# A planned DeltaNet and FFN kernel on one core: the planner learns of the eight transfers that may be open

## The chip, the cores and the metric

The kernel runs on one core of one Trainium2 chip. The metric is the device time of one execution in microseconds. It is given as the median of several runs; the profile is of one execution.

## The reference

Two layers follow each other. The first is a DeltaNet recurrence over 768 steps, for 4 batches of 8 heads of 48 dimensions; the second is a SwiGLU feed-forward network (FFN) without bias on the 3072 resulting tokens of 384 numbers, with 1536 inner columns and an RMS norm ahead of it.

```python
k_n = k / (norm(k) + 1e-6)
for t in range(S):
    y[t] = q[t] @ state
    v_old = state.T @ k_n[t]
    state = state + beta[t] * outer(k_n[t], v[t] - v_old)
x = y.transpose(0, 2, 1, 3).reshape(3072, 384)
xn = x / sqrt(mean(x * x) + 1e-6) * rms_g
out = (silu(xn @ w_gate) * (xn @ w_val)) @ w_out
```

The three weight matrices come in as 64-bit floats, and the kernel turns them into 32-bit ones itself.

## The kernel before

**Work.** The 768 steps are cut into twelve chunks of 64 (`C`). For each chunk `c`, `prep(c)` makes the small triangular matrix that replaces the 64 sequential steps, `qpart(c)` makes the masked scores of queries against keys, and `recur(c)` applies both to the state and gives the chunk's 256 rows of `x`. Then the FFN works on these 256 tokens. Chunks 0 and 1 go through `ffn_plain` (up-products L1083, down-products L1065); chunks 2 to 11 go through `ffn` and `down`, which form the products with fewer multiplications from sums of weight blocks (L1176 and L1233).

**A chunk's chain.** In `prep`, the keys' scores go to DRAM (`dkk`) and come back in another layout as `at`. VectorE (DVE) scales it (L654), takes a first share (L679, L684, L689) and does 15 steps of two instructions (L701 and L707). The result goes to DRAM as `dx`, and for chunks 2 to 11 also as `dxt`, and comes back in four transfers of `x2bd` and eight of `mt`, and for chunks 2 to 11 two of `m1bd`. TensorE (PE) merges the blocks (L783, L807; for chunks 0 and 1 also L759), with short copies by DVE (L772, L823) and ScalarE (ACT) in between; `recur` follows with L894, L908 and L945, DVE's copy L933 and the transposes L1016 that give `xf`, the FFN's input. For chunks 0 and 1 the result lies in `wsum`.

**Weights.** `weights` loads 18 blocks of 768 KB into three raw buffers in `more`; each is turned into 32-bit floats by one ACT instruction (L465) and three or four DVE ones (L453, L456, L461, and L486 where PE doesn't add the parts).

**Order.** Nothing of the order is left to the compiler. Each operation is an `Op` of the class `Plan`, with an engine, a duration, a priority and its dependences. `Plan.run` calls `forward` and `backward` by turns, 60 times (`ROUNDS`), with small random shakes of the priorities from a fixed seed, and keeps the order whose modelled end is the earliest. `forward` is a list scheduler: among the operations whose dependences are met, it takes the one with the earliest start and, among equal starts, the smallest key. `backward` sets the keys anew from the latest times at which each operation may start. The chosen order is then issued; each engine works through its list in order, and what holds it up on the chip are semaphores alone. The modelled times stay behind, with one exception: where PE's plan has a hole before 70 us, `filler` puts matmuls on the identity there (L1333), as many as fill the hole as planned.

**Transfers in the plan.** `dma` adds a transfer to the list of SyncE (SP) or, for a few of chunk 0, of ACT. The model has one `server` for all transfers: each occupies it for its `work`, after those planned ahead of it, and its dependents can start 0.7 us after its end. Some have an `after`, an earliest time in the plan. The work of a weight block is 3.06 us, of a half of `k`, `q` or `v` 1.02, of a half of `at` 1.8, of an `mt` or `x2bd` transfer 0.3. On the chip a transfer's landing is told by one of eight semaphores, which go round over the transfers of SP and ACT together in the order of the list; a transfer that takes a semaphore again waits until the transfer that used it before has landed. The plan before doesn't know that.

**Ports.** `op.port` marks operations of DVE or POOL that, in the model, can't run beside those of the other engine. `Plan.add` sets it false for every operation of SP and ACT.

Of the kernel before, what the change touches and what calls it, by code (L numbers as in the profile page):

```python
# [62 lines left out]
class Plan:  # L63
# [47 lines left out]
    def forward(self, banks, until):  # L111

        at = dict.fromkeys(ENGINES, 0.0)
        held = {"DVE": 0.0, "POOL": 0.0}
        cand = {e: [] for e in ENGINES}
        free = list(banks)
        for op in self.ops:
            op.wait, op.at = len(op.deps), op.ready
            for g in op.acquire:
                g.taken, g.uses = False, g.left  # L120
            if not op.wait:
                cand[op.eng].append(op)
        order, server, end_, mode = [], 0.0, 0.0, 0
        backlog = 0.0
        while len(order) < len(self.ops):
            best = None
            for e in ENGINES:
                for op in cand[e]:
                    s = max(op.at, at[e])
                    if op.port:  # L130
                        s = max(s, held["POOL" if e == "DVE" else "DVE"])
                    n = sum(not g.taken for g in op.acquire)
                    if n > len(free):
                        continue
                    if n:
                        s = max(s, free[n - 1])
                    key = op.key + (STICK if op.mode is not None and op.mode != mode else 0.0)
                    rate, store = (FETCH, AHEAD) if s > EARLY else (FETCH0, AHEAD0)
                    if op.size and backlog + op.size - rate * op.dur > store:
                        key += 2.0 * STICK  # L140
                    if best is None or (s, key, op.n) < best[0]:
                        best = ((s, key, op.n), op)
            if best is None:
                return None
            (s, _, _), op = best
            cand[op.eng].remove(op)
            for g in op.acquire:
                if not g.taken:
                    g.taken = True
                    free.pop(0)  # L150
            op.start = s
            if op.mode is not None and op.mode != mode:
                s += 0.1
                op.start, mode = s, op.mode
            end = s + op.dur
            if op.eng == "PE":
                if s - at["PE"] > 1.4 and s > until:
                    end += 1.6
                rate, store = (FETCH, AHEAD) if s > EARLY else (FETCH0, AHEAD0)
                fill = 6.0 if s < until else 0.0  # L160
                backlog = max(0.0, backlog - (rate - fill) * (s - at["PE"])) + op.size - rate * op.dur
                late = max(0.0, backlog - store) / rate
                backlog, end = max(0.0, backlog - rate * late), end + late
            at[op.eng] = end - min(OVERLAP[op.eng], op.dur)
            if op.port:
                held[op.eng] = end
            end_ = max(end_, end)
            for g in op.release:
                g.uses -= 1
                if not g.uses:  # L170
                    free.append(end + 0.1)
                    free.sort()
            if op.dma:
                server = max(end + 0.9, server) + op.work
                end = server
            op.end = end
            for u in op.users:
                u.wait -= 1
                u.at = max(u.at, at[op.eng] if u.eng == op.eng and not op.dma else end + op.hop(u) + u.slack)
                if not u.wait:  # L180
                    cand[u.eng].append(u)
            order.append(op)
        self.end = end_
        return order
# [65 lines left out]
def kernel(  # L250
# [17 lines left out]
    nc = tc.nc  # L268
# [94 lines left out]
    G = lambda n: 0.15 + 0.0022 * n  # L363

    def dma(dst, src, prio, r=(), w=(), work=0.3, dur=0.5, eng="SP", after=0.0):
        queue = nc.scalar if eng == "ACT" else nc.sync
        op = P.add(eng, dur, lambda: queue.dma_start(out=dst, in_=src), prio, r, w, lat=0.7)
        op.dma, op.work, op.ready = True, work, after

    PERIOD = 51.0  # L370

# [41 lines left out]
    def load_small():  # L413
        for i in range(8):
            src = beta.rearrange("b (y g) (c i t) -> i g (b y) c t", i=2, g=2, t=W)[i // 2 % 2, i % 2]
            dma(beta_b[16 * i : 16 * i + 16], src, 0.5, w=[("beta", i)], work=0.2, after=7.5)
        dma(g_sb, moe_rms_g.rearrange("(t p) -> p t", p=128), 1, w=["g"], after=8.0)
# [6 lines left out]
    def weights():  # L424
# [14 lines left out]
        for n, (dst, src, keys) in enumerate(todo):  # L439
            pr = (30 if n < 9 else CV2) + 0.2 * n  # L440
            i, a = n % NRAW, n % NCV
            parts = dst.shape[1]
            rdst = raw[i].rearrange("p (a c) -> p a c", a=parts)
            dma(rdst, src, (0.1 if n == 0 else 3 + 2 * n), w=[("raw", i)], dur=0.7, work=3.06, after=(7.5, 5.0, 19.2, 27.2, 24.5, 33.3, 47.0)[n] if n < 7 else 48.8)

            low, high = (raw[i].bitcast(U32)[:, w_ : w_ + 2 * WCOL - 1 : 2] for w_ in range(2))
# [922 lines left out]
```

## Time and profile before

| What | Value |
|---|---|
| Median of 3 runs | 712.54 us (712.05 to 716.23) |
| Span of the profiled execution, first to last instruction | 709.8 us |
| Instructions | 23280 |
| PE busy | 700.7 us (99%) |
| DVE busy | 543.5 us (77%) |
| ACT busy | 314.0 us (44%) |
| POOL busy | 139.9 us (20%) |
| Moved by DMA | 54.66 MB, mean 77 GB/s |
| Mean granted TensorE clock | 1.000 |

The profiled execution is a run of its own, for which the page gives the span and no other time; the span lies 2.7 us under the median of the runs. PE's busy time contains the filler, so it doesn't say how much of PE's time is useful. The share of DVE, and that of the DMA engines, is a mean over a first part with much of both and a long rest with little.

### The profile page before, as it was taken

Reading aid. Unit: us, or ns where it says so; the run is one execution under the profiler, and the core shown is the slowest. Engines: PE = TensorE matmul, PEld = TensorE weight load, DVE = VectorE, ACT = ScalarE, POOL = GpSimd, SP = SyncE. Lnnn points to the kernel's source line nnn. Section 1 sums busy time; section 2 is a strip of 40 time slices with the busy share of each in tenths; the row PEclk is TensorE's granted clock in tenths of the full one; section 3 lists DMA queues with packets and bytes.
Section 4 is the critical chain, followed back from the end, with each engine's and each line's share of the span. In section 5 each row is a group of like instructions: output and inputs, shape, how many; then the busy total and the mean of one; then the engine's idle time right before and its main releaser. Section 6 shows DMA issues by size and latency. Waiting matters only on the chain.

```text
span 709.8 us, 23280 instructions
## 1 busy us (share of the span) xinstructions
PE 700.7 (99%) x10040; PEld 637.8 (90%) x10040; DVE 543.5 (77%) x1138; ACT 314.0 (44%) x732; POOL 139.9 (20%) x140
## 2 busy tenths in 40 slices
PE   8999999999999999999999999999999999999997
PEld 5657868778799999999999999999999999999997
DVE  4899989999679759849969769669679547957373
ACT  5435554233245445445444445346345345245241
POOL 4201211103133132233223133133213003000000
PEclk9999999999999999999999999999999999999999
DMA  7878795341451161162542431442430350040000
GB/s 138 221 149 188 180 262 170 51 79 24 75 112 27 33 111 31 28 111 46 90 77 47 74 71 25 90 76 48 78 67 11 56 103 2 15 64 2 23 1 23
DMA packets 210070, 54.66 MB, mean 77 GB/s; under 512 B 199216, under 2 KB 202288, under 8 KB 209968
## 3 DMA queue, kind: packets, MB, share of 16 engines
q1 hardware_dynamic: 205120, 52.26, 36.9%
q10 hardware_dynamic: 4848, 0.92, 0.8%
q8 instruction: 79, 1.29, 0.8%
q14 instruction: 23, 0.19, 0.1%
HBM read 40.83 MB, written 12.32 MB: 75 GB/s over the span
## 4 chain that ended last, share of the span: by engine, by line
PE 91%; DVE 5%; DMA 3%; issue 1%; ACT 1%; POOL 0%; ACTq 0%; POOLq 0%; DVEq 0%
PE bank L1176 39%; PE bank L1233 19%; PE bank L1083 9%; PE bank L1065 4%; PE bank L538 3%; PE bank L848 3%; PE bank L515 3%; PE bank L1333 2%; PE bank L894 2%; PE bank L908 2%; DMA more<-in_moe_w_gate_dram 2%; PE bank L807 2%; DVE acc L707 1%; PE bank L1016 1%; PE bank L945 1%; DVE acc L701 1%
## 5 line engine op out<-in xcount | busy, mean ns | idle before, releaser
L1186 DVE TENSOR_TENSOR tmp<-tmp,bank 128x512 f32<-128x512 f32 x180 | 121.2, 682 | 79.5 <-PE bank L1176 68.5
L1176 PE MATMUL bank<-xf,w_in 128*128 128x128 f32 x1440 | 181.1, 277 | 0.0
L1176 PEld LDWEIGHTS bank<-xf,w_in 128*128 128x128 f32 x1440 | 170.1, 192 | 2.6 <-issue 0.8
L1176 PE MATMUL bank<-xf,more 128*128 128x128 f32 x960 | 125.2, 277 | 0.0
L1176 PEld LDWEIGHTS bank<-xf,more 128*128 128x128 f32 x960 | 115.4, 192 | 2.4 <-issue 0.6
L1188 ACT COPY tmp<-bank 128x512 f32<-128x512 f32 x120 | 69.0, 586 | 78.2 <-PE bank L1176 58.3
L1192 ACT ACTIVATE tmp<-tmp 128x256 f32<-128x256 f32 x120 | 49.9, 417 | 97.9 <-DVE tmp L1186 97.6
L707 DVE TENSOR_REDUCE acc<-acc 128x30 f32<-128x90 f32 (+4 forms) x180 | 85.1, 473 | 6.2
L560 POOL TENSOR_TENSOR knrm<-ksum,half 128x16 f32<-128x16 f32 x12 | 36.2, 3019 | 158.0 <-DVE ksum L559 158.0
L701 DVE TENSOR_TENSOR acc<-acc,at 128x60 f32<-128x60 f32 (+4 forms) x180 | 62.3, 346 | 2.8
L1233 PE MATMUL bank<-wo_sb,hf 128*128 128x192 f32 x360 | 63.7, 327 | 0.0
L1233 PEld LDWEIGHTS bank<-wo_sb,hf 128*128 128x128 f32 x360 | 58.3, 190 | 0.1
L1193 DVE TENSOR_TENSOR hf<-tmp 128x256 f32<-128x256 f32 x120 | 51.0, 437 | 7.7 <-ACT tmp L1192 7.2
L1333 PE MATMUL bank<-ident 128*128 128x128 f32 (+2 forms) x160 | 44.9, 427 | 1.4 <-POOL ident masks.py:199 1.4
L728 POOL COPY acc<-acc 128x128 f32<-128x128 f32 x40 | 21.5, 568 | 123.1 <-DVE acc L707 122.5
L1333 PEld LDWEIGHTS bank<-ident 128*128 128x128 f32 x160 | 27.0, 196 | 17.9 <-issue 15.2
L654 POOL TENSOR_TENSOR at<-at,beta_b 128x1024 f32<-128x1024 f32 x8 | 18.9, 2360 | 85.7 <-DMA at<-dkk 73.7
L1083 PE MATMUL bank<-xf,w_in 128*128 128x256 f32 x144 | 34.6, 385 | 0.9 <-DVE r L862 0.9
L1065 PE MATMUL bank<-wo_sb,hf 128*128 128x384 f32 x96 | 34.6, 491 | 0.0
L1083 PE MATMUL bank<-xp,w_in 128*128 128x256 f32 x144 | 32.8, 380 | 0.0
L1083 PEld LDWEIGHTS bank<-xf,w_in 128*128 128x128 f32 x144 | 26.4, 190 | 6.0 <-DVE r L862 1.5
L1083 PEld LDWEIGHTS bank<-xp,w_in 128*128 128x128 f32 x144 | 27.0, 190 | 4.6
(166 smaller groups left out, 1024.5 us busy)
## 6 DMA issues: line engine op xcount, KB each, us to landing
at<-dkk SPq DMA_DIRECT2D x23, 256.0 KB, 4.2
q<-in_q_dram SPq DMA_DIRECT2D x24, 192.0 KB, 3.7
more<-in_moe_w_val_dram SPq DMA_DIRECT2D x6, 768.0 KB, 6.2
more<-in_moe_w_gate_dram SPq DMA_DIRECT2D x6, 768.0 KB, 7.4
more<-in_moe_w_out_dram SPq DMA_DIRECT2D x6, 768.0 KB, 6.9
vt<-in_v_dram SPq DMA_DIRECT2D x24, 192.0 KB, 4.2
out_dram<-tmp SPq DMA_DIRECT2D x48, 96.0 KB, 2.2
k<-in_k_dram SPq DMA_DIRECT2D x23, 192.0 KB, 3.8
```

The lines of the kernel that those rows point to most:

```text
L560: P.add("POOL", 2.95, lambda: nc.gpsimd.tensor_tensor(out=knrm[i2], in0=ksum[i2], in1=half, op=ALU.pow), pn, r=[("ksum", i2), "half"], w=[ ...
L701: nc.vector.tensor_tensor(out=acc[:, 1:3, 0:n, j + 2 : W].rearrange("p a i t -> p i a t"), in0=acc[:, old, 0:n, j : j + 2, None].to_broadc ...
L707: nc.vector.tensor_reduce(out=acc[:, new, 0:n, j + 2 : W], in_=acc[:, lo : lo + 3, 0:n, j + 2 : W].rearrange("p a i t -> p i t a"), axis=A ...
L1065: nc.tensor.matmul(po[p].t[:, 0:DM], hf[:, spot(f), 128 * p : 128 * p + 128], wo_sb[:, spot(f)], start=(f == f0), stop=(f == f1 - 1), skip ...
L1083: nc.tensor.matmul(ps.t[:, TOK * side : TOK * side + TOK], w_in[:, side, h_, 3 * t + i_, n : n + 128], x_[:, 2 * t : 2 * t + 2].rearrange( ...
L1176: nc.tensor.matmul(g.t[:, 128 * z : 128 * z + 128], fac[:, side, 128 * f : 128 * f + 128], xf[:, xs], start=(begin and z == 0), stop=False ...
L1186: P.add("DVE", V(512), lambda t=t, g=g: nc.vector.tensor_tensor(out=t, in0=t, in1=g.t, op=ALU.add), -1, r=[g], w=[tk], last=g)
L1188: P.add("ACT", A(512), lambda t=t, g=g: nc.scalar.copy(t, g.t), -1, r=[g], w=[tk], last=g)
L1192: P.add("ACT", A(256), lambda t=t: nc.scalar.activation(out=t[:, 0:256], in_=t[:, 0:256], func=ACTF.Silu), -1, w=[tk])
L1193: P.add("DVE", V(256), lambda t=t, f0=f0, p=p: nc.vector.tensor_tensor(out=hf[:, spot(f0) : spot(f0) + 2, 128 * p : 128 * p + 128], in0=t[ ...
L1233: nc.tensor.matmul(g.t[:, 0:192], a_[:, f], b_[:, f], start=(begin and f == 0), stop=(f == 5), skip_group_check=True)
L1333: nc.tensor.matmul(warm[:, 0 : 128 * w_].rearrange("p (w n) -> p w n", n=128), ident, ident[:, None, :].to_broadcast([128, w_, 128]))
```

## The change

`forward` keeps a list of eight times, one for each of the last eight transfers of SP and ACT in the order of planning: the modelled landing plus 0.7 us. A further transfer of SP or ACT can't start in the plan before the oldest of them. `dma` learns of a third queue, POOL, and sets `op.port` false for each transfer; no call in the kernel names that queue. The code that issues instructions is otherwise as it was, and so are all durations, priorities and the seed; the order comes out of the planner anew.

```diff
@@ forward
         order, server, end_, mode = [], 0.0, 0.0, 0
         backlog = 0.0
+        lanes = [0.0] * 8
         while len(order) < len(self.ops):
             best = None
             for e in ENGINES:
                 for op in cand[e]:
                     s = max(op.at, at[e])
+                    if op.dma and e != "POOL":
+                        s = max(s, lanes[0])
                     if op.port:
                         s = max(s, held["POOL" if e == "DVE" else "DVE"])
...
             if op.dma:
                 server = max(end + 0.9, server) + op.work
                 end = server
+                if op.eng != "POOL":
+                    lanes = lanes[1:] + [end + 0.7]
             op.end = end
@@ dma
-        queue = nc.scalar if eng == "ACT" else nc.sync
+        queue = {"ACT": nc.scalar, "SP": nc.sync, "POOL": nc.gpsimd}[eng]
         op = P.add(eng, dur, lambda: queue.dma_start(out=dst, in_=src), prio, r, w, lat=0.7)
-        op.dma, op.work, op.ready = True, work, after
+        op.dma, op.work, op.ready, op.port = True, work, after, False
```

## Prediction

> **What bounds the kernel now.** First the page's busy shares and slices.
>
> ```profile
> PE 700.7 (99%) x10040; PEld 637.8 (90%) x10040; DVE 543.5 (77%) x1138; ACT 314.0 (44%) x732; POOL 139.9 (20%) x140
> PE   8999999999999999999999999999999999999997
> DVE  4899989999679759849969769669679547957373
> ```
>
> TensorE is busy from end to end, so an order can gain only where that busy time isn't useful work. Next, the windows by stage show which engines are full in each (columns: window, length, busy time and count of PE, PE loads, DVE, ACT, POOL; clock; DMA share; GB/s).
>
> ```profile
> 30.00:40.00 10.00, 10.00 (x35) 5.32 (x34) 9.30 (x20) 2.86 (x5) 0.00 (x0) 1.00 0.88 177
> 60.00:70.00 10.00, 9.87 (x285) 8.16 (x284) 9.52 (x26) 7.08 (x23) 1.82 (x3) 1.00 0.94 147
> 100.00:110.00 10.00, 10.00 (x159) 7.14 (x159) 9.38 (x15) 6.66 (x17) 4.52 (x3) 1.00 1.08 250
> 110.00:160.00 50.00, 50.00 (x585) 39.32 (x586) 48.55 (x92) 16.83 (x36) 3.97 (x5) 1.00 0.40 86
> 250.00:300.00 50.00, 50.00 (x823) 48.32 (x822) 40.79 (x88) 24.20 (x58) 13.36 (x13) 1.00 0.30 55
> ```
>
> There are three stages. Until 72 us no FFN product runs; PE's busy time is mostly filler (L1333: 44.9 us of it), while from 20 us on DVE is 89 to 98% busy and the DMA engines 0.62 to 0.94. From 72 to 160 us PE, DVE and, until 110, the transfers are full together. From 160 us PE alone is: the list of PE's waits between 72 and 709 us holds one entry, `PE bank L1083 <- DVE r L862`, 0.9 us.
>
> Third, SyncE's queue where chunk 0's merge transfers go out (start, length, what).
>
> ```profile
> 44.98 0.54 SPq L367 DMA_DIRECT2D more<-in_moe_w_gate_dram  x1
> 46.37 0.96 SPq L367 DMA_DIRECT2D mt<-dx  x2
> 47.46 5.43 SPq L367 DMA_DIRECT2D x2bd<-dx  x2
> 52.93 0.95 SPq L367 DMA_DIRECT2D mt<-dx  x2
> ```
>
> Two issues of `x2bd` span 5.43 us, though the first takes 1.17 and the second 0.30: between them SyncE stands 3.95 us, until 52.59. The weight load of 44.98 landed 7.6 us later, at 52.57. By the trace's semaphores it is the eighth transfer ahead of that second issue; the eight semaphores go round, and by issue and landing times never more than seven earlier transfers are open at an issue. So the limit that the change writes into the planner is real before it, too. Seven of the 427 issues stand on it clearly, with 11.0 us of queue time in all; six of them lie before 81 us, the seventh (0.17 us) at 256 us. Steady chunks hardly meet it.
>
> Fourth, the chain of waits just ahead of the FFN (start, length, what).
>
> ```profile
> 57.97 0.64 PE bank L1333 x4
> 59.61 1.50 PE bank L1333 x8
> 62.96 0.86 PE bank L1333 x6
> 65.52 2.36 PE bank L1333 x10
> 69.31 1.72 PE bank L1333 x8
> 71.36 0.88 PE bank L1333 x6
> 72.23 2.62 PE bank L1083 x12
> ```
>
> 7.96 us of filler stand on the chain itself. The planner puts filler where its plan has PE idle before 70 us; where the chip is ahead of the plan, real work waits behind filler.
>
> **The change part by part.** It adds and removes no instruction on the chip: `dma` is called with SP or ACT alone, so the new POOL key is never used, and `op.port` is already False for such an op, so its new last assignment alters nothing (exactly 0, under no cover). The one live edit makes the earliest start of an SP or ACT transfer in `forward` also wait for `lanes[0]`. All 427 issues stay on their queues; what can differ is the list order of all five engines, and the filler. Four terms:
>
> 1. *The waits themselves.* The chip's waits on the eighth transfer stay, whatever the planner knows. Only another order can move them: from -3.95 us (SyncE's longest one goes) to +3.95 (another like it arises). I take 0: the first-come rule of `forward` still issues the 44.98 load as soon as SyncE is free and the load's `after` has passed, ahead of the `mt` transfers, which are candidates only when `dx` has landed at 46.22. Behind a wait of this sort stand the other `mt`, `x2bd` and the two weight loads at 53.99 and 54.49 on SyncE, and ACT's own conversion of weights (`ACT w_in L483` sat 6.6 us there).
>
> 2. *Filler.* A planned transfer that starts later moves planned PE work later, and the hole is filled. Least: all 7.96 us of the chain's filler go. Most: SyncE's 3.95 us turn wholly into filler. The plan already lets transfers land one after the other; with the 44.98 load's 3.06 us in that line its last `mt` lands late even without the rule, so little is added: I take +1, nearer to the row with no wait than to the 3.95.
>
> 3. *Weight loads and their conversion.* After 72 us PE has one hole, 0.9 us at 94, behind a load issued at 85.07 that landed 7.14 us later. Least -0.9; most +8.45 (a load landing one full turn later; the one issued at 97.33 took that long). I take +1, near the 0.9 row, since what is late next is DVE's conversion, which has 0.6 us free in each 10 there.
>
> 4. *The 550 us after 160.* Here PE's rate matters. In the chain 8 matmuls of L1176 in a row take 1.09 us and 16 take 1.98, so each further eight cost 0.89 and each break 0.20. Two breaks fewer a chunk to four more, over ten chunks: -4 to +8. I take one more, +2.0: an order drawn anew has no reason to have fewer, and DVE (40.79 of 50) and ACT have room to follow it.
>
> Sum: 0 + 1 + 1 + 2 = +4.0 on a span of 709.8, 713.8. The median of the runs (712.54) is 2.7 above that span, so 716.5. The four terms' ends don't come together; half of them on either side gives the likeliest case its own range, 708.5 to 721.
>
> One rule bears on the plan's picture of the queues. The row first: an `mt` transfer of ACT's queue, issued at 46.28 with 32 KB, landed 6.5 us later, just after SyncE's 768 KB; the middle one of all SyncE's `mt` takes 2.2. So ACT's small transfer had to wait for SyncE's big one, as in the planner's single line. The Trainium skill, page "DMA: Bandwidth & Descriptors", section "Queues, rings and completion order", has each DMA engine turn between the queues packet by packet, which speaks against the new rule's one line of landings: a small transfer from ACT need not wait for a long one from SyncE. By the page the planned waits would be too long by the difference, 4.3 us, all of it filler, and my sum 720.8; by the row it stays 716.5, and I go by the row.
>
> **Rivals.**
>
> *A worse place for the conversions: 725.* A weight conversion is four DVE instructions, 0.55 + 0.56 + 0.96 + 0.96 = 3.03 us (L453, L456, L461, L486 at 69 to 73 us). Between 50 and 68 us DVE does chunk 1's steps (L701, L707), and chunk 0's short copies (L772, L823, L933) are threaded among them. If the plan holds that chunk 0's transfers land later, conversions get threaded ahead of the copies; on the chip all of chunk 0's path, and the first FFN product at 72.23, then waits. Three of them give +9.1; with the +4 above, 712.5 + 13.1 = 725.6, say 725. From +7.1 us in all it is over 1%, so two conversions (6.1) with half of the small terms decide it. For it: DVE is over 93% busy there, so nothing moved ahead is free. Against it: the copies' priorities come from the backward pass and are far ahead of the conversions'. Six give 735.
>
> *The rule sorts the queue better: 705.* Where all transfers wait for the same lane, `forward` chooses by priority instead of by arrival. Then `at<-dkk` could go ahead of the weight load at 16.80 (the first `at` on ACT's queue took 7.2 us to land, the ordinary ones 4.2: 3.0 us) and chunk 0's `mt` ahead of the load at 44.98 (52.57 instead of 49.94, when the second `at` landed: 2.6), and half of the filler goes (4.0): 9.6 us. But DVE's windows from 20 to 110 us add up to 82.4 of 90: 7.6 us free is all that an earlier start can use before DVE is the bound. 712.5 - 7.6 = 705. For it: that cap is not below the bar of 1%. Against it: it needs nearly all of DVE's idle time, and the transfers at 100 us are full as well.
>
> *It does nothing: 712.5.* If the rule never binds on the plan's best order, list and filler stay. Against it: the plan's line has the same burst of twelve transfers at 46 us behind the same long load.
>
> **How the numbers follow.** Likeliest case 0.42 (of it 0.02 over the bar of 1% on the slow side), misplaced conversions 0.38, better sorting 0.16, nothing 0.04. The slow rival is given nearly as much as the likeliest because three of the four terms can lose more than they can gain, and the full DVE before 160 us gives misplaced work back to the end. One per cent, about what a measurement of this kernel can tell from no change, is 705.4 to 719.7: faster 0.16, same 0.42 - 0.02 + 0.04 = 0.44, slower 0.38 + 0.02 = 0.40. The range holds 8 in 10 from 704.5, just under the fast rival, to 733, which leaves out the slow rival's worst, with more than five conversions.
>
> **What would show it.** The first L1083 product should start at 72 to 75 us; at 80 or later the slow rival is true, at 65 the fast one. L1333's 44.9 us of filler should be 44 to 48. PE's idle after 100 us should stay under 1 us, and the busy time of L1176 within 4 us of now. SyncE should still show a stall of 2 to 5 us among chunk 0's `mt` and `x2bd`. The forecast is wrong if PE gets holes of over 1 us between 110 and 200 us, or if a steady chunk comes to take over 1 us more than now.

## The result, and the profile after

The changed kernel takes 718.16 us (median of 4 runs, 716.65 to 722.23) against 712.29 for the kernel before: a ratio of 1.0083, 95% interval 1.0055 to 1.0111. It is slower by 0.8%, within the bar of 1%. The profiled execution of the changed kernel is its slowest, 722.23 us with a span of 719.6; so some 4 of the 9.8 us between the two spans are that run's own, and what matters is what returns in other runs.

The page's busy shares and slices:

```profile
PE 703.8 (98%) x10028; PEld 638.5 (89%) x10028; DVE 547.5 (76%) x1138; ACT 313.0 (43%) x732; POOL 141.4 (20%) x140
PE   8898899999999999999999999989999999999997
DVE  4889789999699859669679569749739949848373
PEclk9999899999999999999999999999999999999999
```

PE's row has dents that it lacked, and the granted clock one at 72 to 90 us. The windows (length, busy time and count of PE, PE loads, DVE, ACT, POOL; clock; DMA share; GB/s) place them:

```profile
60.00:70.00 10.00, 9.25 (x312) 7.80 (x315) 9.46 (x25) 4.86 (x16) 2.31 (x1) 1.00 0.60 141
70.00:80.00 10.00, 5.95 (x44) 4.37 (x36) 9.79 (x15) 6.76 (x20) 3.98 (x4) 0.68 0.70 149
250.00:300.00 50.00, 50.00 (x827) 48.59 (x826) 38.99 (x88) 23.98 (x58) 12.96 (x13) 1.00 0.34 62
450.00:500.00 50.00, 47.99 (x792) 46.10 (x791) 35.66 (x80) 21.77 (x54) 11.21 (x11) 0.97 0.37 67
```

From 70 to 80 us PE has 4 us without work while DVE is full, and the clock is 0.68 on average. SyncE's queue, by contrast, looks as before:

```profile
44.41 0.54 SPq L372 DMA_DIRECT2D more<-in_moe_w_gate_dram  x1
45.78 0.83 SPq L372 DMA_DIRECT2D mt<-dx  x2
47.12 4.76 SPq L372 DMA_DIRECT2D x2bd<-dx  x2
52.27 0.80 SPq L372 DMA_DIRECT2D mt<-dx  x2
```

The same load is issued ahead of the same transfers, and the second `x2bd` waits for it again, 4.16 us by the issue times (3.95 before). The planner knows of the wait now and takes it all the same. Where the time goes is seen on DVE. First before, then after (start, length, what):

```profile
55.93 0.48 DVE L707 TENSOR_REDUCE acc<-acc 128x96 f32<-128x288 f32 x1
56.33 0.84 DVE L772 COPY m1bd<-bank 32x256 f32<-32x256 f32 x2
57.20 0.39 DVE L701 TENSOR_TENSOR acc<-acc,at 128x220 f32<-128x220 f32 x1
```

```profile
56.29 0.48 DVE L712 TENSOR_REDUCE acc<-acc 128x96 f32<-128x288 f32 x1
...
58.73 0.40 DVE L777 COPY m1bd<-bank 32x256 f32<-32x256 f32 x1
...
60.13 0.42 DVE L777 COPY m1bd<-bank 32x256 f32<-32x256 f32 x1
```

Lines are five higher after the change; L777 is L772. Before, chunk 0's two copies go out together behind the fourth step of chunk 1. After, the first goes behind the sixth and the second behind the seventh, and PE's merge needs both: 60.55 instead of 57.17 us, 3.4 us. That is no wait for transfers: all eight `mt` had landed by 55.0 us, and PE's matmuls that the copies read were done at 55.7. The chain of waits goes on like this:

```profile
68.58 0.07 DVE ms L993
...
69.85 0.47 DVE more L458
70.32 0.07 DVE ms L993
...
72.93 0.92 ACT more L470
73.86 0.63 ACT yn L1008 x2
74.48 0.04 issue
74.53 0.92 PE bank L1021 x3
75.44 0.02 issue
75.47 0.38 ACT xf L1025
75.84 0.04 issue
75.89 5.06 PE bank L1088 x12
```

Weight conversions (L458 on DVE, L470 on ACT) stand ahead of chunk 0's last pieces, and the first FFN products, twelve matmuls that took 2.62 us before, take 5.06: they run at half the clock. In windows of 2 us the clock is 1.00 until 72, 0.89, then 0.50 from 74 to 80.

To see how the loss grows, I counted for each matmul its mean spacing in the profile of before, filler as nothing, and read when so much useful PE work was issued:

| Useful PE work, us | before at | after at | later by |
|---|---|---|---|
| 15 | 43.8 | 44.2 | 0.4 |
| 18 | 57.3 | 60.7 | 3.4 |
| 25 | 72.6 | 77.0 | 4.4 |
| 28 | 75.7 | 81.8 | 6.1 |
| 100 | 149.0 | 154.7 | 5.8 |
| 400 | 448.7 | 453.1 | 4.4 |
| 500 | 548.4 | 557.6 | 9.2 |
| 600 | 648.1 | 657.9 | 9.8 |

So 3.4 us come with the copies. The first product starts 3.7 us later (75.89 against 72.23), and the twelve products at half the clock add 2.4 (5.06 against 2.62): together the 6.1 at 28 us. The row at 25 us lies within these products. Chunk 0's own path lost more than that. First before, then after:

```profile
65.24 0.73 ACT L1003 ACTIVATE yn<-bank,rs 128x192 f32<-128x192 f32 x2
66.59 0.73 ACT L1003 ACTIVATE yn<-bank,rs 128x192 f32<-128x192 f32 x2
```

```profile
72.17 0.73 ACT L1008 ACTIVATE yn<-bank,rs 128x192 f32<-128x192 f32 x2
73.76 0.71 ACT L1008 ACTIVATE yn<-bank,rs 128x192 f32<-128x192 f32 x2
```

Its scaled rows end 7 us later. Some 3.6 us of that lie behind the copies: POOL's key norm (L565, 67.69 to 70.96 us) stands ahead of chunk 0's roots, and the pieces above stand ahead of the rows. Before, PE came to its rows only at 67.7 and 70.9 us, behind filler, so that the first product shows no more than 3.7 of the 7.

Later some of the loss is won back, and this run loses 5 us more after 400, where PE has one hole of 2.0 us and one of 0.8, and the clock falls to 0.50 for 3 us behind the first. About half of these 5 us returns elsewhere: counted in the same way, the profiles of three runs below that keep this part of the list (the old start with the new rest, the filler in the holes, POOL alone reordered) lose 2.5 to 2.7 us between 400 and 600, without the 2.0 us hole and at a clock of 1.00.

### The profile page after: what moved, and what is told of

It reads as the page before. It is cut to its first block, busy times and chain, and to the rows that moved or that the text cites. A ratio compares the mean times of both kernels' runs of the same rounds, so it can differ in the third digit from the quotient of the medians.

```text
span 719.6 us, 23217 instructions
## 1 busy us (share of the span) xinstructions
PE 703.8 (98%) x10028; PEld 638.5 (89%) x10028; DVE 547.5 (76%) x1138; ACT 313.0 (43%) x732; POOL 141.4 (20%) x140
## 4 chain that ended last, share of the span: by engine, by line
PE 84%; DVE 9%; issue 2%; POOL 2%; DMA 1%; ACT 1%; SPq 1%; ACTq 0%; POOLq 0%; DVEq 0%
PE bank L1181 35%; PE bank L1238 19%; PE bank L1088 7%; PE bank L1070 4%; PE bank L543 3%; PE bank L853 3%; PE bank L1338 3%; PE bank L520 2%; DVE acc L712 2%; DVE acc L706 1%; PE bank L812 1%; PE bank L913 1%; PE bank L899 1%; PE bank L1021 1%; PE bank L788 1%
## 5 line engine op out<-in xcount | busy, mean ns | idle before, releaser
L1191 DVE TENSOR_TENSOR tmp<-tmp,bank 128x512 f32<-128x512 f32 x180 | 121.2, 684 | 81.0 <-PE bank L1181 74.1
L1181 PE MATMUL bank<-xf,w_in 128*128 128x128 f32 x1440 | 180.1, 277 | 2.0 <-ACT tmp L1193 2.0
L1181 PE MATMUL bank<-xf,more 128*128 128x128 f32 x960 | 126.3, 279 | 0.8 <-DVE tmp L1191 0.8
L565 POOL TENSOR_TENSOR knrm<-ksum,half 128x16 f32<-128x16 f32 x12 | 37.0, 3082 | 235.9 <-DVE ksum L564 235.9
L1338 PE MATMUL bank<-ident 128*128 128x128 f32 (+2 forms) x148 | 43.2, 439 | 1.4 <-POOL ident masks.py:199 1.4
L1338 PEld LDWEIGHTS bank<-ident 128*128 128x128 f32 x148 | 24.9, 196 | 18.4 <-issue 16.1
L1088 PE MATMUL bank<-xf,w_in 128*128 128x256 f32 x144 | 36.7, 404 | 0.5 <-ACT xf L1025 0.5
L1247 DVE TENSOR_TENSOR tmp<-tmp,bank 128x192 f32<-128x192 f32 x30 | 10.5, 350 | 31.2 <-PE bank L1238 31.2
L1088 PEld LDWEIGHTS bank<-xf,w_in 128*128 128x128 f32 x144 | 28.1, 201 | 6.3 <-ACT xf L1025 0.9
L1088 PE MATMUL bank<-xp,w_in 128*128 128x256 f32 x144 | 33.2, 381 | 0.3 <-DVE hf L1096 0.3
```

The source lines that it names most:

```text
L565: P.add("POOL", 2.95, lambda: nc.gpsimd.tensor_tensor(out=knrm[i2], in0=ksum[i2], in1=half, op=ALU.pow), pn, r=[("ksum", i2), "half"], w=[ ...
L1088: nc.tensor.matmul(ps.t[:, TOK * side : TOK * side + TOK], w_in[:, side, h_, 3 * t + i_, n : n + 128], x_[:, 2 * t : 2 * t + 2].rearrange( ...
L1181: nc.tensor.matmul(g.t[:, 128 * z : 128 * z + 128], fac[:, side, 128 * f : 128 * f + 128], xf[:, xs], start=(begin and z == 0), stop=False ...
L1191: P.add("DVE", V(512), lambda t=t, g=g: nc.vector.tensor_tensor(out=t, in0=t, in1=g.t, op=ALU.add), -1, r=[g], w=[tk], last=g)
L1338: nc.tensor.matmul(warm[:, 0 : 128 * w_].rearrange("p (w n) -> p w n", n=128), ident, ident[:, None, :].to_broadcast([128, w_, 128]))
```

## The experiments

Two theories stood against each other. **The rule**: orders planned with knowledge of the eight transfers are late on the chip. **The draw**: `Plan.run` keeps the best of 60 shaken rounds, and any edit of the planner draws 60 others; the loss is the luck of this draw. Beside that, the start had to be told from the rest, and the pieces of the start from each other.

**Other draws.** The only edit is the seed, in the changed planner or in the one before:

```diff
-        rng = random.Random(47)
+        rng = random.Random(46)   # 62; without the rule: 45, 57
```

The modelled ends of 24 seeds, which the planner itself works out, run from 701.0 to 708.4 us without the rule and from 702.9 to 708.2 with it; the seed in use gives 701.2 and 704.7, so it is a good draw in the first and a middling one in the second. The other seeds that were run are the two with the earliest modelled end in each planner.

> The planner with the new rule, but the shakes of its 60 rounds drawn from seed 46 instead of 47. The planner's own modelled end is 702.9 us instead of 704.7, and its first FFN product stands at 71.0 us instead of 73.6. Theory 'the draw' (the rule costs little, the one order drawn with seed 47 is a late one): first FFN product at 73 to 74 us, time 713 to 715. Theory 'the rule' (planning with the rule gives late orders on the chip): first product at 75 us or later, time 717 or more.

> The planner before, without the rule, seed 45: modelled end 701.0 us (701.2 with 47), first FFN product at 69.7 us in both. It shows how far one draw differs from another on the chip. Theory 'the draw': 711 to 717, a spread of the size of the loss. Theory 'the rule': 711 to 713.5, like before.

> The planner with the new rule and seed 62: modelled end 702.9 us, first FFN product planned at 70.5. Theory 'the draw': between 711 and 716, no worse than the orders drawn without the rule. Theory 'the rule': 716 or more.

> The planner before, without the rule, seed 57: modelled end 701.1 us, first FFN product planned at 69.7. Theory 'the draw': 711 to 717, as seed 45 gave 716.3 and the kernel before 712.5. Theory 'the rule': 711 to 714.

| Planner | Seed | Modelled end | Ratio to before, 95% interval |
|---|---|---|---|
| without the rule | 47 (before) | 701.2 | 1 |
| without | 45 | 701.0 | 1.0041 (1.0021 to 1.0061) |
| without | 57 | 701.1 | 0.9975 (0.9958 to 0.9991) |
| with the rule | 47 (the change) | 704.7 | 1.0083 (1.0055 to 1.0111) |
| with | 46 | 702.9 | 1.0044 (1.0020 to 1.0069) |
| with | 62 | 702.9 | 1.0036 (1.0016 to 1.0057) |

Draws without the rule differ by 0.66% from each other, nearly as much as the whole change, though their modelled ends agree within 0.2 us. That is the draw, shown. With the rule two other seeds lose about half of what seed 47 loses. The mean is 1.0005 without the rule and 1.0054 with it, but the two groups overlap (1.0041 against 1.0036), and three draws each can't show that the rule by itself costs anything. Both theories were too sharp: with 715.53 us for seed 46 and 715.09 for seed 62, "717 or more" and "716 or more" were wrong, and so were "713 to 715" for seed 46 and, in the mean, "no worse than the orders drawn without the rule".

The first product of seed 46, planned for 71.0 us, came at 78.6 in the profile, for a reason that no order holds. Of PE's waits:

```profile
PE bank L950 <- issue: 3.1, 1, 3.1
```

PE stopped for 3.1 us in the middle of 64 matmuls with nothing to wait for but its own instructions.

**Which part of the list.** The kernel plans twice and joins the lists: the first up to a time of its plan, then what is left in the order of the second.

```diff
+        a = self.best_order(free, until, lanes=False)   # start_after: True; after_to_53: True
+        b = self.best_order(free, until, lanes=True)    # start_after: False; after_to_53: False
+        head = [... ops of a with a start before 150.0]  # after_to_53: 53.0
+        return head + [... ops of b that are not in head]
```

> The kernel plans twice, without and with the rule, and issues the first plan's list up to its 150 us, then what is left in the second plan's order. Theory 'the start' (all that counts is the lost 5.6 us before 150 us): 712 to 713.5. Theory 'start and rest' (the profiled run lost a further 4.2 us after 400 us): 714 to 717.

> The same the other way round: the list planned with the rule up to 150 us, then the rest in the order planned without it. Theory 'the start': 717 to 719. Theory 'start and rest': 715 to 717, with no holes in PE after 150 us.

> The list planned with the rule up to 53 us of its plan, the rest in the order planned without it. Theory 'the loss of the start comes from the order after 53 us, beginning with DVE's copies into m1bd behind more steps of chunk 1': first FFN product at 72 to 73 us, time 712 to 714. Theory 'the transfers' order before 53 us makes it' (other places of x2bd and mt in the queues): 716 or more.

With the changed start and the old rest: 718.85 us, ratio 1.0086 (1.0056 to 1.0116), the whole loss. With the old start and the new rest: 715.69, 1.0041 (1.0028 to 1.0054); in its profile 2.0 us of the loss come where the lists are joined. The first result is what 'the start' expected, the second what 'start and rest' expected. Together they are more than the change, so part of the second is the joint's; the start alone is enough to account for the result, and that the rest costs something too isn't ruled out. With the new list up to 53 us only: 712.89, 1.0006 (0.9987 to 1.0026), nothing lost, though in its profile the first product came at 74.30, later than expected. Up to 53 us the planner's two lists differ almost only in the places of transfers, and these cost nothing; the chip's wait stands in that run too, with 4.5 us, so it doesn't account for the loss. The loss is made from 53 to 150 us. There the order of the transfers differs as well as that of the engines, and no run moved the copies alone; that it begins with DVE's copies is read from the traces:

```profile
57.26 0.84 DVE L791 COPY m1bd<-bank 32x256 f32<-32x256 f32 x2
```

Here both copies go out together again (L791 is L772 of before).

**The clock.** Filler in PE's two holes at 70 to 75 us of the changed order, into unused columns of a bank that is held anyway:

```diff
+HOLES = {251: 10, 261: 4}     # ahead of the two groups of L1021
...
+            if op.n in HOLES:
+                filler([1] * HOLES[op.n], spare, 384)
             op.fn()
```

> The changed kernel's order, with filler matmuls of 128 columns put into the two holes that PE had at 70 to 75 us (ten and four, into unused columns of a held PSUM bank); nothing else moves. Theory 'the clock' (PE's idle time there let the granted clock fall to 0.68 for 70 to 80 us, which made the first FFN products take twice their time): the clock stays at 1.00, the first twelve products take 2.6 us instead of 5.06, time 715 to 717. Theory 'the clock costs nothing' (products later wait for weights anyway): no change, 717.5 to 719.

716.22 us, 1.0050 (1.0032 to 1.0069): 0.0033 of the 0.0083, some 2.4 us, is won back. The two intervals overlap, so the size is rough; but the mean granted clock tells all the runs apart: 0.992 to 0.997 in the four of the changed kernel, 0.998 to 1.000 in the ten of this one. The first twelve products now run at a clock of 1.00, though the profiled execution is the slowest of the ten, 718.76 us (L1093 is L1088):

```profile
71.90 1.72 PE L1343 MATMUL bank<-ident 128*128 128x128 f32 x13
73.92 0.94 PE L1343 MATMUL bank<-ident 128*128 128x128 f32 x7 [0.31 <-issue]
74.70 0.49 PE L1026 MATMUL bank<-ident,yn 128*128 128x128 f32 x3
75.03 1.06 PE L1343 MATMUL bank<-ident 128*128 128x128 f32 x8
76.09 0.55 PE L1026 MATMUL bank<-ident,yn 128*128 128x128 f32 x3
77.10 2.94 PE L1093 MATMUL bank<-xf,w_in 128*128 128x256 f32 x12 [0.46 <-ACT xf L1030]
```

In this profile PE started its products even later, at 77.1, so an earlier start isn't what was won. The changed kernel stops its filler at the plan's 70 us, a fixed number that suited a first product planned for 69.7 and doesn't suit one planned for 73.6.

**Chunk 0's last pieces.** In the changed order, other work on POOL, or on POOL and ACT, is put behind them:

```diff
+        # after_pool: key norm of chunk 2 behind the roots; acc's clearing behind the rows L1008
+        for n, behind in ((333, 258), (390, 260), (389, 260)):
+        # after_pool_act: a conversion (81, and on DVE 82, 83) and the clearing behind xf too
+        for n, behind in ((333, 258), (83, 264), (82, 264), (81, 264), (390, 264), (389, 264)):
+            move op n right behind op `behind` in the list
```

> The changed kernel's order, with three instructions groups moved: on POOL the key norm of chunk 2 (L565) behind both root instructions of chunk 0 (L1000), on ACT the clearing of acc (L664, L670) behind chunk 0's scaled rows (L1008). Theory 'POOL and ACT hold chunk 0 back': L1008 starts at 70.4 instead of 72.2, the first FFN product at 74 instead of 75.9, PE's holes shrink and the clock stays higher; time 714 to 716.5. Theory 'DVE alone sets it' (all was lost with the late copies on DVE before 66 us): 717 to 719.

> The changed kernel's order with chunk 0's last pieces put first at 68 to 74 us: on POOL the key norm of chunk 2 behind chunk 0's two roots, and on ACT one weight conversion (its L465) and the clearing of acc behind chunk 0's scaled rows and xf (its L1003 and L1020); that conversion's next two DVE steps move with it. Theory 'other work was threaded ahead of chunk 0's last pieces': the second scaled rows at 71 to 72 us instead of 73.8, first FFN product at 73 to 74 instead of 75.9, clock 1.00; time 713.5 to 716. Theory 'DVE's late copies alone': 717 to 719.5, as the kernel with POOL alone reordered.

Both failed as cures: 719.45 us, 1.0096 (1.0062 to 1.0130), and 719.62, 1.0089 (1.0067 to 1.0110). In the first, POOL's root came 2.2 us earlier and the first group of rows with it, but ACT then stood at the conversion, which waits for DVE, ahead of the second, and the first product came at 76.63 us:

```profile
72.55 0.89 ACT L478 ACTIVATE more<-more 128x768 f32<-128x768 f32 x1 [1.89 <-DVE w_in L499]
73.33 0.72 ACT L1016 ACTIVATE yn<-bank,rs 128x192 f32<-128x192 f32 x2
```

In the second, the first product did come at 74.1 instead of 75.9, but the clock, expected at 1.00, was 0.59 and 0.56 from 74 to 78 us, and the gain was given back at once, in the chunk that follows:

```profile
75.68 0.17 DVE L576 TENSOR_SCALAR knrm<-knrm 128x16 f32<-128x16 f32 x1 [1.81 <-POOL knrm L573]
```

```profile
PE bank L528 <- DVE pt L591: 2.7, 1, 2.7
```

DVE itself now waits for the delayed key norm, does the conversions behind it, and comes late to the instruction (L591) that PE waits for. By 35 us of useful work this kernel is 9.2 us behind the one before, where the changed one is 6.7. Moving one piece turns its wait into another's.

**A version that beats both, by little.** The prediction had found 7.96 us of filler on the chain of before. From its plan's 64.5 us on the filler is left out; in the second run ACT's clearing of `acc` is also moved behind chunk 0's `xf`.

```diff
-                if s < until:
+                if s < 64.5:
                     filler(fillers(pe, s))
...
+        for n, behind in ((390, 264), (389, 264)):   # second run only
+            move op n right behind op `behind` in the list
```

> The kernel before, without the filler that its plan places from 64.5 us on (ten, eight and six matmuls between 65.5 and 72.2 us in the profile). In the profile of before L1003's rows are ready at 66.0 and 67.3 us, while L1016 starts at 67.7 and 70.9 behind filler. Theory 'filler holds real work up': the first FFN product at 69 to 70 us instead of 72.2, the clock stays (PE's holes stay under 1.5 us), time 709.5 to 711. Theory 'the clock needs the filler': the clock falls near 70 us, time 713 or more. If the rest of the start is bound by the weights: 712 to 713.

> The kernel before without its filler from 64.5 us of the plan on, and with ACT's clearing of acc behind chunk 0's last xf rows (its L1020), which waited for it in the run with less filler alone. If PE's start sets the end: first FFN product at 69 us instead of 70.98, time 709 to 711. If the conversions on DVE set it: 711.5 to 713.5.

Without the filler alone: 713.81 us, 1.0011 (0.9993 to 1.0030), no difference. The profiled execution is one of its fastest, 710.73 us at a mean clock of 1.000; there the first product came at 70.98, held by the clearing on ACT:

```profile
PE bank L1083 <- ACT xf L1020: 2.9, 1, 2.9
```

The other executions tell more. The three with a mean granted clock of 0.999 or 1.000 took 710.27 to 712.31 us, the nine with 0.994 to 0.998 took 712.92 to 715.59. So the median falls on the side of the theory 'the clock needs the filler', which the profile alone seems to contradict; that the clock falls at 70 us in those nine is likely, but no profile shows one of them.

With both edits: the first product at 68.36, 3.9 us earlier than before, and 711.92 us, 0.9981 (0.9968 to 0.9994). PE's hole ahead of the first product is 1.0 us instead of 2.9, and the mean clock is 0.997 to 1.000 in all twelve runs. What the second edit wins in the ratio, 0.0030 or some 2 us, may thus be the clock alone: at a mean clock of 0.999 or more the first edit by itself is about as fast. The version is better than before by 1.4 us, no change by the bar of 1%, and than the change by 1.0%. Of the 3.6 us that this run is ahead at 25 us of useful work, 0.8 are left at 50: PE waits for keys and for DVE meanwhile. The other version that beats both is the draw with seed 57, without the rule, 711.02 us.

## Why the prediction was right, and where its steps were not

The forecast was 716.5 us, no change by the bar of 1%, and 718.16 lies in the likeliest case's own range. Its sum was right to 1.7 us, its terms were not; that the sum came so close is luck.

- *The waits themselves, 0*: right. The chip's wait stayed (4.16 us against 3.95), the load kept its place ahead of `mt`, and the list up to 53 us costs nothing.
- *Filler, +1*: wrong in sign and kind. Filler fell from 44.9 to 43.2 us, under the 44 to 48 that was set as a mark; its price lay not in too much of it but in its end at the plan's 70 us while the first product moved past it. The prediction took the clock as given and had no term for it; it measured some 2.4 us.
- *Weight loads, +1*: wrong in sign and small. The hole of 0.9 us at 94 us is gone.
- *The rate after 160 us, +2*: wrong. The busy time of L1176 was 306.3 us before and 306.4 after (180.1 + 126.3). Counted in the traces from 160 us on, its matmuls stand in 88 stretches before and in 90 after: two more breaks, not ten. The price of a break was read high, too: in the chain of before, a stretch of eight from 160 us on takes 0.89 us more often than 1.09. Much of what this stage lost in the profiled run it lost in two holes of PE and the clock behind one. The mark of under 1 us of idle time of PE after 100 us was missed there, with 3.1.
- *What was missing*: the place of short copies on the full DVE, 3.4 us at 57 us by the traces, the largest single piece of what PE loses up to its first products. It was in the rival of the misplaced conversions, whose place was right and whose price was not: steps of chunk 1 went ahead of the copies, not three conversions, 3.4 us instead of 9.1. The argument against it, that the copies' priorities are far ahead of the conversions', has nothing on chunk 1's steps, and these went ahead. Conversions did stand ahead of chunk 0's last pieces at 70 to 74 us. The first product at 75.9 us fell between the marks set for the likeliest case (72 to 75) and for this rival (80).
- *The rival of better sorting* asked for earlier `at` and `mt` transfers; the load ahead of chunk 0's `mt` kept its place. Its cap, DVE's few idle microseconds, fits the last run: 3.9 us at the first product became 1.4 at the end.
- *No hole of over 1 us between 110 and 200 us*: held. *A steady chunk not over 1 us slower*: held from 100 to 400 us of useful work, where the changed kernel won back 1.4 us, and missed after that: from 400 to 500 the profiled run lost 4.8.

The row that was set against the skill's rule of queues that turn packet by packet wasn't tested by an experiment of its own. The changed kernel's trace has the same row: ACT's `mt` issued at 46.35 us landed at 52.25, 5.9 us later and just after SyncE's load (51.56).

## What to carry to other kernels

A planner's order is a draw: three orders with modelled ends within 0.2 us differed by 0.66% on the chip, so an edit of the planner has to be judged over several seeds, or it is judged by its luck. A constant tuned to one plan (here the end of the filler at 70 us) is part of that plan; when a change moves what it was tuned to, look at it first. Where one engine is over 90% busy, read its list to see what goes ahead of the short instructions that another engine waits for, and expect a piece that is moved forward there to be paid for by the next. Look at the granted clock of every run and not only of the profiled one: with less filler the profile showed a clock of 1.00, and nine runs of twelve had a mean of 0.994 to 0.998.

## What the runs showed of the hardware that was not expected

- **The clock follows holes, not their length alone.** A hole of 2.0 us of PE at 477 us was followed by a granted clock of 0.50 for about 3 us; four microseconds of idle time in three pieces at 70 to 76 by 0.50 from 74 to 80:

```profile
478.00:479.00 1.00, 0.00 (x0) 1.00 0.43 66
480.00:481.00 1.00, 1.00 (x6) 0.50 0.45 69
```

But in the profiled execution with less filler one hole of 2.94 us left the clock at 1.00, and nine of the twelve executions of that order had a mean clock of 0.994 to 0.998, as told above. The Trainium skill, "TensorE: Matmul & The Clock Gate", section "Part 1: The HAM clock gate (the 'warmup' mystery)", says that the clock is halved after an idle window of about 3.4 us that runs freely. The half agrees with the trace; the 2.0 us hole is shorter than such a window, so the measurement goes beyond the page's figure. A free-running window may be why one order keeps its clock in some executions and not in others, which no run here shows.
- **PE can stop for its own instructions.** Besides the 3.1 us above, the changed kernel stopped 1.5 us at 25.7 us inside a run of 64 small matmuls; both times nothing else released it. In the trace's transfer records a block of 16 KB of the instruction queue falls into or next to each of the two holes, while the DMA engines' share is over 0.7. Such a block comes every 9 us on average (78 in 719.6 us), so this says little, and that the loaded DMA engines delay those blocks is inferred, not shown.
- **One program's runs differ by about 1%** in this kernel: the 10 runs with seed 46 lie between 713.17 and 719.91 us. The six with a mean granted clock of 0.999 or 1.000 take 713.17 to 716.27, the four with 0.997 or 0.998 take 717.46 to 719.91; so what costs the clock comes and goes between runs of one order. Whether it is holes like these, one profile can't show.
